# A planner that orders one fused kernel's operations by passes from the front and from the back in turn

## The chip, the cores and the metric

The kernel runs on one core of a Trainium2 chip. The metric is the device time of one execution in microseconds. A core has five engines with an instruction stream each: TensorE (PE; its weight loads are listed as PEld), VectorE (DVE), ScalarE (ACT), GpSimd (POOL) and SyncE (SP). SP issues all transfers here. Each engine works through its stream in order, and a semaphore wait holds up whatever stands behind it on that engine.

## The reference

Three stages follow each other. All are in 32-bit floats at the end; the kernel gets weights as 64-bit floats and splits them.

```python
# attention: 4 batches, 8 heads, 576 tokens, head size 64, window of 64 tokens
scores = (1 / 8) * q @ k.T            # kept where 0 <= i - j < 64
attn = exp(scores - max); attn = attn / (sum(attn) + 1e-9)
x = attn @ v                          # 2304 tokens x 512
# first block, 512 -> 2048 -> 512
h = x @ w_in
g = (a0 + a1 h + a2 h^2 + a3 h^3) / (1 + |b0| |h| + |b1| h^2 + 1e-6)
x = g @ w_out
# second block, 512 -> 1024 -> 1024 -> 512
out = (((x @ w1) * (x @ w2)) @ w3) @ w_out2
```

## The kernel before, in words

Tokens are cut into six blocks of 384 (index j). Attention runs in 48 steps of one token range and one pair of heads; a step multiplies scores (S, L516), masks and reduces them on VectorE (L519), takes the exponential on ScalarE (L525), scales each row by the reciprocal sum (nm, L530 on ScalarE or, in the first eight steps, L532 on GpSimd), transposes (T, L537), copies the transposed tile (ac, L541) and multiplies by v (O, L482); the result is split into two parts of fewer bits for TensorE (L487, L490).

The first block runs over 48 pairs of 128-wide chunks of its 2048 inner columns: product H (L600), the rational function on ScalarE and VectorE (L612 to L671), product D into the four accumulators of the token block (L677). Each product is three matmuls of split parts. The chunk pairs go through the halves of the inner columns in a fixed order of turns (L247): blocks 0, 1, 2 with the first half, then 2, 1, 0 with the second, then blocks 3 to 5 with both.

Every weight tile arrives as 64-bit floats in 512 KB (`conv`, load L378), is converted by three bit operations on VectorE (L382, L385, L388), and is split by ScalarE (L395) and VectorE (L398). The second block has the products AB (L843), a product of its last two weights W (L878), its result for the first token pair (L1129), and for the other two token pairs products P and R by a scheme of seven block products (L1029, L1174).

None of these loops sets the order in which engines work. Each operation is registered with a planner (class `Plan`, L33): a key, the engines that may do it with a planned cost for each ("E" TensorE, "V" VectorE, "A" ScalarE, "P" GpSimd, "D" the transfer queue), the operations that it follows, the buffers that it takes or uses, and a `tail`, the planned delay until its result can be used. `order` (L70) turns these into one sequence:

1. Due times are worked out backwards over the dependences from a nominal sequence of TensorE's products (`seq`), by costs, tails and a lag between engines.
2. In each buffer ring the values are ordered by those due times (L111), and each new value has to follow the users of the value whose buffer it takes.
3. Due times are worked out again with these dependences, and the operations are placed by one pass from the front: whenever an engine is free in the plan, it takes the ready operation that is due first. VectorE's operations marked `port` and all of GpSimd's exclude each other.

The operations are then issued in the order of their planned starts. The chip keeps each engine's order, but starts each instruction when its semaphores allow, so the plan's times themselves are not used on the chip. An operation of "D" occupies the planned transfer queue for its cost, one after the other, and its result is usable a tail later.

Of the kernel before, what the change touches and what calls it, by code (L numbers as in the profile page):

```python
# [19 lines left out]
P = 128  # L20
B, H, S, D = 4, 8, 576, 64
# [18 lines left out]
class Plan:  # L40
# [29 lines left out]
    def order(self):  # L70
        ops, n = self.ops, len(self.ops)
        preds = [[(self.index[k], True) for k in o["after"]] for o in ops]

        def topo():
            left = [len(p) for p in preds]
            succs = [[] for _ in ops]
            for i, p in enumerate(preds):
                for j, _ in p:
                    succs[j].append(i)
            out = [i for i in range(n) if not left[i]]  # L80
            for i in out:
                for j in succs[i]:
# [12 lines left out]
        def lag(i, j):  # L95
            a, b = ops[i]["engines"][0][0], ops[j]["engines"][0][0]
            return self.SAME[a] if a == b else self.CROSS

        def dues():
            out, succs = topo()  # L100
            due = [1e9] * n
            for i in reversed(out):
                d = min([due[j] - lag(i, j) - ops[i]["engines"][0][1] - ops[i]["tail"] for j in succs[i]], default=1e9)
                due[i] = d if ops[i]["due"] is None else min(d, ops[i]["due"])
            return due

        due = dues()

        tags = {}
        for v, (a, users) in self.values.items():  # L110
            tags.setdefault(v[0], []).append((due[a] if ops[a]["turn"] is None else ops[a]["turn"], a, users))  # L111
        for tag, vs in tags.items():
            vs.sort()
            for k in range(1, len(vs)):
                preds[vs[k][1]].append((vs[k - 1][1], False))
                if k >= self.rings[tag]:
                    preds[vs[k][1]] += [(u, True) for u in vs[k - self.rings[tag]][2]]
        due = dues()
        _, succs = topo()
        left = [len(p) for p in preds]  # L120
        ready_at = [0.0] * n
        free = {}
        pend, ready = {}, {}
        for o in ops:
            for e, _ in o["engines"]:
                free[e] = 0.0
                pend[e], ready[e] = [], []
        start = [None] * n
        events = [0.0]

        def release(i):
            for e, _ in ops[i]["engines"]:
                heappush(pend[e], (ready_at[i], i))
            heappush(events, ready_at[i])

        for i in range(n):
            if not left[i]:
                release(i)
        port = 0.0
        while events:  # L140
            t = heappop(events)
            for e in free:
                while pend[e] and pend[e][0][0] <= t:
                    i = heappop(pend[e])[1]
                    if start[i] is None:
                        heappush(ready[e], (due[i], i))
            while True:
                best = None
                for e in free:
                    if free[e] > t:  # L150
                        continue
                    kept = []
                    while ready[e]:
                        d, i = ready[e][0]
                        if start[i] is not None:
                            heappop(ready[e])
                        elif port > t and self.ports(ops[i], e):
                            kept.append(heappop(ready[e]))
                        else:
                            if best is None or d < best[0]:  # L160
                                best = (d, i, e)
                            break
                    for x in kept:
                        heappush(ready[e], x)
                if best is None:
                    break
                _, i, e = best
                o = ops[i]
                o["engine"], start[i], free[e] = e, t, t + dict(o["engines"])[e]
                heappush(events, free[e])  # L170
                if self.ports(o, e):
                    port = free[e]
                for j in succs[i]:
                    left[j] -= 1
                for j in set(succs[i]):
                    real = any(r for k, r in preds[j] if k == i)
                    ej = ops[j]["engines"][0][0]
                    d = free[e] + o["tail"] + (self.SAME[e] if e == ej else self.CROSS) if real else t + 1e-6
                    ready_at[j] = max(ready_at[j], d)
                    if not left[j]:  # L180
                        release(j)
        assert all(s is not None for s in start)
        self.start = start
        return [ops[i] for i in sorted(range(n), key=lambda i: (start[i], i))]
# [3 lines left out]
def body(ctx: ExitStack, tc: tile.TileContext, qkv, w_in, w_out, a, b, w1, w2, w3t, wo2, out):  # L188
# [43 lines left out]
    op = plan.op  # L232
# [134 lines left out]
    def conv(name, dst, n, src, tag, due=None, spare=False, pre=None, kept=None):  # L367
# [40 lines left out]
        op((name, n, "load"), (("D", 1.55),), load, after=["swap"] if spare else [], new=(ws,), tail=2.2, due=due)  # L408
# [6 lines left out]
        else:  # L415
            op((name, n, "hi"), (("A", 0.52),), hi, after=((name, n, "b2"),), uses=(wt, ws))
            op((name, n, "lop"), (("V", 0.61),), lo, port=True, after=((name, n, "hi"),), uses=(wt, ws), due=pre + 30.0)
            op((name, n, "keep"), (("D", 1.55),), keep, after=((name, n, "lop"),), uses=(ws,), tail=2.0, due=pre + 31.0)
            op((name, n, "lo"), (("D", 1.55),), again, after=((name, n, "keep"),), new=(wc,), tail=2.2)
# [14 lines left out]
        op((name, n, "keepb"), (("D", 0.8),), keepb, after=((name, n, "b2"),), uses=(wt,), tail=2.0, due=None if pre is None else pre + 30.5)  # L434
        op((name, n, "keepw"), (("D", 1.55),), keepw, after=((name, n, "lo"),), uses=(wc,), tail=2.0)
# [20 lines left out]
    def attn(pair):  # L456
# [35 lines left out]
        def step(k):  # L492
# [51 lines left out]
            op(("load", i), (("D", 1.0),), load, new=(kb_, qb), tail=2.2)  # L544
            op(("loadv", i), (("D", 0.6),), loadv, after=(("load", i),), new=(vb,), tail=2.2)
# [33 lines left out]
    for m in range(2):  # L579
        after = [("xl", i) for i in range(0, 2 * NP, 2) if i % NP // 2 == m]  # L580
        op(("spill", m), (("D", 2.4),), lambda _, m=m: spill(m), after=after, uses=(("x0", 0),), tail=2.2, due=seq["H", HALF - 2, 0])
        after, xb = [("spill", m)] + [("fill", 0)] * m, ("x0", AGAIN)
        op(("fill", m), (("D", 2.4),), lambda _, m=m: fill(m), after=after, new=() if m else (xb,), uses=(xb,) if m else (), tail=2.2)
# [140 lines left out]
    def evacuate(j, part, then):  # L724
# [30 lines left out]
        for n in range(NK):  # L755
# [8 lines left out]
            if more:  # L764
                after.append(("evl", j, n // 2))
                if n % 2 == 0:
                    op(("evl", j, n // 2), (("D", 1.2),), lambda _, n=n: load(n), after=(("store", j, 0, n), ("store", j, 0, n + 1)), new=(vb,), tail=2.2)
            new = new and not more
            op(("ev", *key), (("A", 0.48), ("V", 0.46))[more:], lambda e, n=n: copy(n, e), after=after, new=(vb,) if new else (), uses=((f"acc{n}", (j, part)),) + (() if new else (vb,)), due=due)
            op(("store", *key), (("D", 0.6),), lambda _, n=n: store(n), after=(("ev", *key),), uses=(vb,), tail=2.0)  # L770
# [33 lines left out]
    def x2_load(j):  # L804
# [15 lines left out]
        for n in range(NK):  # L820
            eb = ("xe", ("x2", j, n))
            after = [("store", j, int(j < HALVED), n), "swap"] + ([("x2l", j, n - 1)] if n else [])
            op(("x2l", j, n), (("D", 0.6),), lambda _, n=n: load(n), after=after, new=(eb,) if n else (eb, xb), uses=(xb,) if n else (), tail=2.2)
# [115 lines left out]
    def tokens(u):  # L939
# [24 lines left out]
        for i, (b, (k, h)) in enumerate(where.items()):  # L964
            j = 2 * u + h
            op(("xl2", u, b), (("D", 1.2),), lambda _, b=b: load(b), after=["swap2"] + [("store", j, int(j < HALVED), n) for n in (2 * k, 2 * k + 1)], new=(fb[b],), tail=2.2, turn=seq["P", u, 0, 1] - 20.0 + i)
        seven((u,), f, fb, {b: ("xl2", u, b) for b in where}, split)

    def weights(u, n):
# [34 lines left out]
        for i in range(4 if u > 1 else 2):  # L1004
            after = [(("w1", "w2")[i], n, "keepw")] if i < 2 else [("keeps", n, i - 2)]
            op(("sw", u, n, i), (("D", 1.55),), lambda _, i=i: load(i), after=after, new=(wbs[i],), tail=2.2)
        if u > 1:
            return
        op(("bs", n), (("D", 1.55),), loadb, after=(("w1", n, "keepb"), ("w2", n, "keepb")), new=(bb,), tail=2.2)
        for i in range(4):  # L1010
            op(("sum", n, i), (("V", 0.34),), lambda _, i=i: sums(i), port=True, after=[("sum", n, i - 1)] if i else [("bs", n)], new=() if i else (sb,), uses=(bb, sb) if i else (bb,))
        for q in range(2):
# [3 lines left out]
            op(("keeps", n, q), (("D", 1.55),), lambda _, q=q: keep(q), after=(("sw", u, n, 2 + q),), uses=(wb,), tail=2.0)  # L1016
# [103 lines left out]
    def result0(h):  # L1120
# [23 lines left out]
        for n in range(NK):  # L1144
            pb, sb = (f"acc{n}", ("R0", h, n)), ("wt", ("so", h, n))
            op(("so", h, n), (("A", 0.45),), lambda _, n=n: copy(n), after=(("R0", h, 3, n),), new=(sb,), uses=(pb,), due=seq["R0", h, 3, n] + 2.0)
            op(("out", h, n), (("D", 0.6),), lambda _, n=n: store(n), after=(("so", h, n),), uses=(sb,), tail=2.0)

    def result(u):
# [53 lines left out]
        for n in range(2):  # L1203
# [5 lines left out]
            for t, half, h, k in (("p1", 0, 0, "p1"), ("u2", 0, 1, "c12"), ("p1b", 1, 0, "p1b"), ("u3", 1, 1, "c22")):  # L1209
                op(("out", u, n, t), (("D", 0.6),), lambda _, t=t, half=half, h=h, n=n: store(t, n, half, h), after=(K(k, n),), uses=(tb(t, n),), tail=2.0)  # L1210
# [79 lines left out]
```

## Time and profile before

| | us |
|---|---|
| median of 3 runs (lowest, highest) | 843.84 (842.42, 844.37) |
| the profiled execution | 843.9 |
| its span, first to last instruction | 842.0 |
| TensorE busy in the span | 811.6 |
| VectorE busy | 679.5 |
| ScalarE busy | 539.8 |

Busy time is the union of an engine's instruction times. The span is what the views of the trace cover, and the time of the run is longer by what lies before and after it. A wait is put down to the instruction that ended last before the waiting one could start. Granted clock 1.00 means TensorE's full clock, 2.4 GHz, and 0.50 half of it.

### The profile page before, as it was taken

How to read it: one execution, taken by the hardware profiler on the slowest of the kernel's cores; microseconds unless marked ns; L12 is line 12 of the kernel's file. 1: busy time of each engine (PE TensorE's matmuls, PEld its weight loads, DVE VectorE, ACT ScalarE, POOL GpSimd, SP SyncE). 2: the span in 40 equal slices, each digit the busy share in tenths (PEclk: the TensorE clock that was granted, in tenths of full speed). 3: DMA queues.
4: the chain of work that ended last, by engine and by line, in shares of the span. 5: the costliest groups of instructions: out<-in, count | busy, mean ns of one | idle time of the engine just before them, and what ended most of it. 6: DMA issues, size and time to landing. Idle time of an engine off the chain costs nothing.

```text
span 842.0 us, 14037 instructions
## 1 busy us (share of the span) xinstructions
PE 811.6 (96%) x5088; PEld 784.0 (93%) x5088; DVE 679.5 (81%) x1333; ACT 539.8 (64%) x1213; POOL 31.7 (4%) x42
## 2 busy tenths in 40 slices
PE   5699989999999999999999999999999999999998
PEld 4589979899999999999999999999889999999998
DVE  6789999999977799888889999889857358933554
ACT  6799888677777978778758685333444335542334
POOL 2100000000001000000000002000000000000000
PEclk9699999999999999999999999999999999999999
DMA  7985472341305354212107856945336589537802
GB/s 243 290 293 162 131 221 100 113 132 47 123 20 164 122 184 159 67 53 89 51 11 249 304 188 224 290 161 192 128 112 236 181 293 307 203 120 252 302 3 76
DMA packets 61285, 138.81 MB, mean 165 GB/s; under 512 B 6944, under 2 KB 36640, under 8 KB 61216
## 3 DMA queue, kind: packets, MB, share of 16 engines
q1 hardware_dynamic: 61216, 137.92, 49.3%
q8 instruction: 40, 0.66, 0.3%
q14 instruction: 29, 0.24, 0.1%
HBM read 102.24 MB, written 35.65 MB: 164 GB/s over the span
## 4 chain that ended last, share of the span: by engine, by line
PE 73%; DVE 16%; ACT 4%; DMA 4%; issue 2%; POOL 1%; SPq 0%; DVEq 0%; ACTq 0%; POOLq 0%
PE acc L677 17%; PE hp L600 14%; PE ab L843 7%; PE pb L1029 6%; PE wp L878 5%; PE pc L1029 4%; PE pa L1029 4%; PE po L1129 4%; PE pb L1174 3%; PE sp L516 3%; PE pc L1174 2%; PE pa L1174 2%; DVE qa L661 2%; DVE wt L385 1%; DVE wt L388 1%
## 5 line engine op out<-in xcount | busy, mean ns | idle before, releaser
L600 PE MATMUL hp<-x,wc 128*128 128x384 f32 x1152 | 219.5, 339 | 1.4 <-DVE x L490 0.4
L677 PE MATMUL acc<-g,wc 128*128 128x384 f32 x1152 | 211.9, 337 | 6.1 <-DVE g L671 3.5
L677 PEld LDWEIGHTS acc<-g,wc 128*128 128x128 f32 x1152 | 198.8, 188 | 11.1 <-DVE g L671 5.0
L600 PEld LDWEIGHTS hp<-x,wc 128*128 128x128 f32 x1152 | 198.9, 188 | 3.7 <-ACT bl L633 2.0
L617 ACT ACTIVATE qa<-hp,cb 128x384 f32<-128x384 f32 x96 | 55.7, 580 | 55.3 <-PE hp L600 54.3
L622 ACT ACTIVATE u<-hp,ca 128x384 f32<-128x384 f32 x96 | 64.9, 676 | 5.9 <-PE hp L600 5.9
L395 ACT ACTIVATE wc<-wt 128x512 fp32r<-128x512 f32 x68 | 42.5, 632 | 40.9 <-DVE wt L388 40.7
L843 PE MATMUL ab<-x,wc 128*128 128x384 f32 x384 | 67.8, 334 | 0.0
L843 PEld LDWEIGHTS ab<-x,wc 128*128 128x128 f32 x384 | 66.7, 188 | 0.0
L525 ACT ACTIVATE sm<-sm,st 128x128 f32<-128x128 f32 x144 | 56.6, 399 | 11.8 <-DVE st L519 11.2
L637 DVE SCALAR_TENSOR_TENSOR qa<-h,cab,qa 128x768 f32<-128x768 f32 x48 | 48.9, 1019 | 15.2 <-ACT h L612 15.1
L1029 PE MATMUL pb<-xb,wc 128*128 128x384 f32 x288 | 56.3, 334 | 0.0
L516 PE MATMUL sp<-k,q 128*128 128x128 f32 x288 | 44.1, 304 | 12.6 <-DMA k<-in_qkv 7.4
L516 PEld LDWEIGHTS sp<-k,q 128*128 128x128 f32 x288 | 41.2, 216 | 13.9 <-DVE st L519 4.5
L641 ACT ACTIVATE r<-qa,cq 128x768 f32<-128x768 f32 x48 | 45.2, 942 | 13.8 <-DVE qa L637 10.2
L1040 DVE TENSOR_TENSOR u<-u,pc 128x384 f32<-128x384 f32 x32 | 17.7, 552 | 43.6 <-ACT u L1037 32.0
L1029 PEld LDWEIGHTS pb<-xb,wc 128*128 128x128 f32 x288 | 50.5, 188 | 0.0
L385 DVE SCALAR_TENSOR_TENSOR wt<-ws,wt 128x512 uint32<-128x512 uint32 x72 | 49.3, 688 | 0.5
L388 DVE SCALAR_TENSOR_TENSOR wt<-ws,wt 128x512 uint32<-128x512 uint32 x72 | 49.3, 686 | 0.3
L612 ACT ACTIVATE h<-hp 128x384 f32<-128x384 f32 x96 | 46.7, 486 | 2.9 <-DVE u L625 2.9
L398 DVE TENSOR_TENSOR wc<-wt,wc 128x512 fp32r<-128x512 f32 x68 | 46.3, 684 | 1.2 <-ACT wc L395 1.2
L1110 DVE TENSOR_TENSOR rt<-prod,rt 128x768 fp32r<-128x768 f32 x36 | 34.3, 954 | 15.0 <-ACT rt L1107 14.9
(97 smaller groups left out, 1344.6 us busy)
## 6 DMA issues: line engine op xcount, KB each, us to landing
wc<-kw SPq DMA_DIRECT2D x48, 512.0 KB, 5.0
kw<-wc SPq DMA_DIRECT2D x32, 512.0 KB, 5.6
q<-in_qkv SPq DMA_DIRECT2D x48, 192.0 KB, 3.3
v<-in_qkv SPq DMA_DIRECT2D x48, 192.0 KB, 3.0
ws<-in_w_in SPq DMA_DIRECT2D x16, 512.0 KB, 4.3
ws<-in_w_out SPq DMA_DIRECT2D x16, 512.0 KB, 4.3
ws<-in_w SPq DMA_DIRECT2D x16, 512.0 KB, 4.4
ws<-in_w3t SPq DMA_DIRECT2D x16, 512.0 KB, 4.3
```

The source lines that it names most:

```text
L385: stt(out=x["b"], in0=x["st"][:, :, 0], scalar=29, in1=x["b"], op0=ALU.logical_shift_right, op1=ALU.bitwise_or)
L388: stt(out=x["b"], in0=x["st"][:, :, 1], scalar=0xC0000000, in1=x["b"], op0=ALU.bitwise_and, op1=ALU.bitwise_or)
L516: nc.tensor.matmul(sp[:, w, :], x["q"][:, w], x["k"][:, w * W_:w * W_ + P], start=True, stop=True)
L525: act(x["sm"][:, m, :], x["sm"][:, m, :], AF.Exp, bias=col(0, k, m), scale=-1.0, accum_out=col(1, k, m))
L600: nc.tensor.matmul(x["hp", m], win[f0 + m][:, s_, kk * P:(kk + 1) * P], (xh, xl)[m_][xk][:, kk, :], start=(kk == 0 and i == 0), stop=(kk = ...
L617: act(x["qa"][:, m, :], x["hp", m], AF.Abs, scale=b0)
L622: act(x["u"][:, m, :], x["hp", m], AF.Identity, scale=a3, bias=a2)
L637: stt(out=x["qa"], in0=x["h2"], scalar=b1, in1=x["qa"], op0=MUL, op1=ADD)
L677: nc.tensor.matmul(accs[j, part, n], wout[f0 + m][:, s_, n * P:(n + 1) * P], x["g"][:, m_, m, :], start=(first and i == 0), stop=(last and ...
L843: nc.tensor.matmul(x[m], w_[n][:, s_, kk * P:(kk + 1) * P], x2[j][m_][:, kk, :], start=(kk == 0 and i == 0), stop=(kk == NK - 1 and i == 2))
L1029: nc.tensor.matmul(x[m], sws[u, n, i0][:, s_, (c0 + k) * P:(c0 + k + 1) * P], t[:, m_, k, :], start=(first and k == 0 and i == 0), stop=(k ...
L1174: nc.tensor.matmul(x[m, n], w[:, s_, (c + n) * P:(c + n + 1) * P], rts[u, b, r][:, m_, k, :], start=(first and r == 0 and k == 0 and i == ...
```

## The change

`order` gets an argument `rounds` of 16. Due times and the buffer order are worked out as before. Then a pass from the front is made as before, and in each round a pass from the back: the same placing routine on reversed dependences, with each operation on the engine that the pass from the front gave it, taking first the operation that ended last. Its mirrored start times become the due times of the next pass from the front. Of the 17 passes from the front, the one with the shortest planned length gives the order and the engines. Beside that, the planned costs of the transfers are changed, all by about a tenth.

```diff
-    def order(self):
+    def order(self, rounds=16):
...
+        first = dues(base)
+        preds = buffers(lambda a: first[a] if ops[a]["turn"] is None else ops[a]["turn"])
+        due = dues(preds)
+        best = None
+        for r in range(rounds + 1):
+            _, succs = topo(preds)
+            start, took = run(preds, succs, due)
+            end = [s + dict(o["engines"])[e] for o, s, e in zip(ops, start, took)]
+            length = max(e + o["tail"] for o, e in zip(ops, end))
+            if best is None or length < best[0]:
+                best = length, start, took
+            self.trail = getattr(self, "trail", []) + [length]
+            if r == rounds:
+                break
+            back, _ = run(succs, preds, [-e for e in end], took)
+            due = [-b - dict(o["engines"])[e] for o, b, e in zip(ops, back, took)]
+        _, self.start, took = best
...
-        op((name, n, "load"), (("D", 1.55),), load, after=["swap"] if spare else [], new=(ws,), tail=2.2, due=due)
+        op((name, n, "load"), (("D", 1.72),), load, after=["swap"] if spare else [], new=(ws,), tail=2.2, due=due)
...
-            op(("load", i), (("D", 1.0),), load, new=(kb_, qb), tail=2.2)
-            op(("loadv", i), (("D", 0.6),), loadv, after=(("load", i),), new=(vb,), tail=2.2)
+            op(("load", i), (("D", 1.1),), load, new=(kb_, qb), tail=2.2)
+            op(("loadv", i), (("D", 0.66),), loadv, after=(("load", i),), new=(vb,), tail=2.2)
```

The other transfers follow the same pattern: 512 KB from 1.55 to 1.72, the two-tile loads and stores of a token block from 2.4 to 2.6, 384 KB from 1.2 to 1.3, 256 KB from 0.8 to 0.88, 192 KB from 0.6 to 0.66. The two constants stay at 0.95, and so do all tails and all engine costs.

## Rows read from the trace of the kernel before

**Rows 1.** Page, part 1: busy us, share of the span, instructions
```profile
PE 811.6 (96%) x5088; PEld 784.0 (93%) x5088; DVE 679.5 (81%) x1333; ACT 539.8 (64%) x1213; POOL 31.7 (4%) x42
```

**Rows 2.** Busy time by stretch, columns in the first row
```profile
core 0: us, PE busy (x) PEld busy (x) DVE busy (x) ACT busy (x) POOL busy (x), PEclk, DMA share, GB/s
0.00:21.00 21.00, 12.02 (x84) 9.89 (x84) 13.19 (x52) 13.05 (x46) 4.86 (x17) 1.00 0.76 243
21.00:42.00 21.00, 14.17 (x108) 11.81 (x108) 15.94 (x58) 14.91 (x53) 3.30 (x5) 0.67 0.94 290
42.00:63.00 21.00, 19.14 (x141) 16.92 (x142) 18.50 (x53) 20.28 (x63) 1.98 (x2) 0.92 0.83 294
63.00:210.00 147.00, 140.74 (x945) 134.96 (x944) 145.65 (x307) 119.32 (x287) 9.89 (x10) 1.00 0.40 129
...
253.00:337.00 84.00, 82.99 (x621) 79.98 (x620) 72.51 (x177) 70.52 (x188) 5.96 (x6) 1.00 0.47 158
...
463.00:547.00 84.00, 83.26 (x478) 82.36 (x477) 80.43 (x124) 51.54 (x92) 5.69 (x2) 1.00 0.76 251
...
631.00:673.00 42.00, 40.87 (x235) 40.62 (x235) 23.60 (x45) 18.86 (x34) 0.00 (x0) 1.00 0.62 210
...
800.00:842.00 42.00, 38.53 (x223) 38.21 (x221) 20.86 (x27) 16.23 (x26) 0.00 (x0) 0.99 0.11 39
```

**Rows 3.** VectorE's waits, 0 to 63 us: total us, times, longest
```profile
DVE wt L382 <- DMA ws<-in_w_out: 3.4, 1, 3.4
...
DVE wt L382 <- DMA ws<-in_w_in: 2.0, 1, 2.0
DVE sm L519 <- ACT wc L395: 1.9, 1, 1.9
DVE u L625 <- ACT u L622: 1.7, 1, 1.7
DVE u L628 <- ACT h L612: 0.4, 1, 0.4
```

**Rows 4.** TensorE's waits, 63 to 210 us
```profile
PE acc L677 <- DVE g L671: 2.5, 4, 1.1
PE acc L677 <- POOL g L671: 1.7, 2, 1.2
PE op L482 <- DVE st L519: 1.1, 1, 1.1
```

**Rows 5.** Timelines of VectorE and TensorE: start, us, instruction, [idle before]
```profile
23.91 0.43 DVE L382 TENSOR_SCALAR wt<-ws 128x512 uint32<-128x512 uint32 x1 [3.39 <-DMA ws<-in_w_out]
...
24.87 1.62 PE L516 MATMUL sp<-k,q 128*128 128x128 f32 x6 [4.42 <-DVE st L519]
```

**Rows 6.** Timeline of the transfer queue, first and last of 23 issues
```profile
0.74 0.39 SPq L502 DMA_DIRECT2D q<-in_qkv  x1
...
16.76 0.38 SPq L378 DMA_DIRECT2D ws<-in_w_out  x1
```

**Rows 7.** Chain that ended last, one piece: start, us, what
```profile
16.76 7.13 DMA ws<-in_w_out
```

**Rows 8.** Busy time by 4 us windows, columns as in Rows 2
```profile
8.00:12.00 4.00, 1.44 (x6) 1.35 (x6) 3.79 (x14) 2.22 (x9) 0.23 (x1) 1.00 0.99 344
...
28.00:32.00 4.00, 3.25 (x18) 2.48 (x19) 2.09 (x4) 3.54 (x12) 1.54 (x2) 0.50 0.96 256
...
48.00:52.00 4.00, 3.23 (x16) 2.14 (x15) 3.17 (x7) 4.00 (x16) 0.00 (x0) 1.00 1.06 369
```

**Rows 9.** Scalings on GpSimd, and TensorE's waits for them
```profile
L532 POOL TENSOR_SCALAR sm<-sm,st 128x128 f32<-128x128 f32 x10 | 6.1, 622 | 27.1 <-DVE st L475 18.6 <-DVE st L519 8.5
...
PE tp L537 <- POOL sm L532: 1.8, 4, 0.7
```

More of the change, by code (lines that the diff above doesn't have):

```diff
@@ L93, in topo, with lag, dues @@
             return out, succs
[L95 to L100, printed above, removed]
+        def lag(i, j, e=None):
+            a, b = e or ops[i]["engines"][0][0], ops[j]["engines"][0][0]
+            return ops[i]["tail"] + (self.SAME[a] if a == b else self.CROSS)
+        def dues(preds):
+            out, succs = topo(preds)
             due = [1e9] * n
@@ L102, in dues @@
             for i in reversed(out):
-                d = min([due[j] - lag(i, j) - ops[i]["engines"][0][1] - ops[i]["tail"] for j in succs[i]], default=1e9)
+                d = min([due[j] - lag(i, j) - ops[i]["engines"][0][1] for j, _ in succs[i]], default=1e9)
                 due[i] = d if ops[i]["due"] is None else min(d, ops[i]["due"])
             return due
[L107 to L148, printed above, removed]
-                for e in free:
[L150 to L158, printed above, removed]
-                        else:
[L160 to L181, printed above, removed]
@@ L182, in order, with buffers @@
-        assert all(s is not None for s in start)
-        self.start = start
-        return [ops[i] for i in sorted(range(n), key=lambda i: (start[i], i))]
+        def buffers(due):
+            preds = [list(p) for p in base]
+            tags = {}
+            for v, (a, users) in self.values.items():
+                tags.setdefault(v[0], []).append((due(a), a, users))
+            for tag, vs in tags.items():
+                vs.sort()
+                for k in range(1, len(vs)):
+                    preds[vs[k][1]].append((vs[k - 1][1], False))
+                    if k >= self.rings[tag]:
+                        preds[vs[k][1]] += [(u, True) for u in vs[k - self.rings[tag]][2]]
+            return preds
@@ new lines, in run, with release @@
+        def run(preds, succs, due, fixed=None):
+            left = [len(p) for p in preds]
+            ready_at = [0.0] * n
+            free, pend, ready = {}, {}, {}
+            for o in ops:
+                for e, _ in o["engines"]:
+                    free[e] = 0.0
+                    pend[e], ready[e] = [], []
+            start, took = [None] * n, [None] * n
+            events = [0.0]
+            def release(i):
+                for e, _ in ops[i]["engines"] if fixed is None else ((fixed[i], 0),):
+                    heappush(pend[e], (ready_at[i], i))
+                heappush(events, ready_at[i])
+            for i in range(n):
+                if fixed is not None:
+                    ready_at[i] = ops[i]["tail"]
+                if not left[i]:
+                    release(i)
+            port = 0.0
+            while events:
+                t = heappop(events)
+                for e in free:
+                    while pend[e] and pend[e][0][0] <= t:
+                        i = heappop(pend[e])[1]
+                        if start[i] is None:
+                            heappush(ready[e], (due[i], i))
+                while True:
+                    best = None
+                    for e in free:
+                        if free[e] > t:
+                            continue
+                        kept = []
+                        while ready[e]:
+                            d, i = ready[e][0]
+                            if start[i] is not None:
+                                heappop(ready[e])
+                            elif port > t and self.ports(ops[i], e):
+                                kept.append(heappop(ready[e]))
+                            else:
+                                if best is None or d < best[0]:
+                                    best = (d, i, e)
+                                break
+                        for x in kept:
+                            heappush(ready[e], x)
+                    if best is None:
+                        break
+                    _, i, e = best
+                    cost = dict(ops[i]["engines"])[e]
+                    took[i], start[i], free[e] = e, t, t + cost
+                    heappush(events, free[e])
+                    if self.ports(ops[i], e):
+                        port = free[e]
+                    for j, real in succs[i]:
+                        left[j] -= 1
+                        if fixed is None:
+                            d = free[e] + lag(i, j, e) if real else t + 1e-6
+                        else:
+                            d = free[e] + lag(j, i, fixed[j]) if real else free[e] - dict(ops[j]["engines"])[fixed[j]] + 1e-6
+                        ready_at[j] = max(ready_at[j], d)
+                        if not left[j]:
+                            release(j)
+            assert all(s is not None for s in start)
+            return start, took
@@ L187, in body @@
+        _, self.start, took = best
+        for o, e in zip(ops, took):
+            o["engine"] = e
+        return [ops[i] for i in sorted(range(n), key=lambda i: (self.start[i], i))]
 @with_exitstack
@@ L417, in conv @@
             op((name, n, "lop"), (("V", 0.61),), lo, port=True, after=((name, n, "hi"),), uses=(wt, ws), due=pre + 30.0)
[L418 to L419 removed]
+            op((name, n, "keep"), (("D", 1.72),), keep, after=((name, n, "lop"),), uses=(ws,), tail=2.0, due=pre + 31.0)
+            op((name, n, "lo"), (("D", 1.72),), again, after=((name, n, "keep"),), new=(wc,), tail=2.2)
         if kept is None:
@@ L580, in body @@
         after = [("xl", i) for i in range(0, 2 * NP, 2) if i % NP // 2 == m]
-        op(("spill", m), (("D", 2.4),), lambda _, m=m: spill(m), after=after, uses=(("x0", 0),), tail=2.2, due=seq["H", HALF - 2, 0])
+        op(("spill", m), (("D", 2.6),), lambda _, m=m: spill(m), after=after, uses=(("x0", 0),), tail=2.2, due=seq["H", HALF - 2, 0])
         after, xb = [("spill", m)] + [("fill", 0)] * m, ("x0", AGAIN)
-        op(("fill", m), (("D", 2.4),), lambda _, m=m: fill(m), after=after, new=() if m else (xb,), uses=(xb,) if m else (), tail=2.2)
+        op(("fill", m), (("D", 2.6),), lambda _, m=m: fill(m), after=after, new=() if m else (xb,), uses=(xb,) if m else (), tail=2.2)
     win, wout, accs = {}, {}, {}
@@ L822, in x2_load @@
             after = [("store", j, int(j < HALVED), n), "swap"] + ([("x2l", j, n - 1)] if n else [])
-            op(("x2l", j, n), (("D", 0.6),), lambda _, n=n: load(n), after=after, new=(eb,) if n else (eb, xb), uses=(xb,) if n else (), tail=2.2)
+            op(("x2l", j, n), (("D", 0.66),), lambda _, n=n: load(n), after=after, new=(eb,) if n else (eb, xb), uses=(xb,) if n else (), tail=2.2)
             op(("x2h", j, n), (("A", 0.45),), lambda _, n=n: hi(n), after=(("x2l", j, n),), uses=(eb, xb))
@@ L965, in tokens @@
             j = 2 * u + h
-            op(("xl2", u, b), (("D", 1.2),), lambda _, b=b: load(b), after=["swap2"] + [("store", j, int(j < HALVED), n) for n in (2 * k, 2 * k + 1)], new=(fb[b],), tail=2.2, turn=seq["P", u, 0, 1] - 20.0 + i)
+            op(("xl2", u, b), (("D", 1.3),), lambda _, b=b: load(b), after=["swap2"] + [("store", j, int(j < HALVED), n) for n in (2 * k, 2 * k + 1)], new=(fb[b],), tail=2.2, turn=seq["P", u, 0, 1] - 20.0 + i)
         seven((u,), f, fb, {b: ("xl2", u, b) for b in where}, split)
@@ L1146, in result0 @@
             op(("so", h, n), (("A", 0.45),), lambda _, n=n: copy(n), after=(("R0", h, 3, n),), new=(sb,), uses=(pb,), due=seq["R0", h, 3, n] + 2.0)
-            op(("out", h, n), (("D", 0.6),), lambda _, n=n: store(n), after=(("so", h, n),), uses=(sb,), tail=2.0)
+            op(("out", h, n), (("D", 0.66),), lambda _, n=n: store(n), after=(("so", h, n),), uses=(sb,), tail=2.0)
     def result(u):
@@ L1209, in result @@
             for t, half, h, k in (("p1", 0, 0, "p1"), ("u2", 0, 1, "c12"), ("p1b", 1, 0, "p1b"), ("u3", 1, 1, "c22")):
-                op(("out", u, n, t), (("D", 0.6),), lambda _, t=t, half=half, h=h, n=n: store(t, n, half, h), after=(K(k, n),), uses=(tb(t, n),), tail=2.0)
+                op(("out", u, n, t), (("D", 0.66),), lambda _, t=t, half=half, h=h, n=n: store(t, n, half, h), after=(K(k, n),), uses=(tb(t, n),), tail=2.0)
     for n in range(NG):
```

26 lines of the change are left out of this document (14 added, 12 removed).

## The prediction, made before the changed kernel ran

> **What bounds the kernel now.** I read the engine shares first, then the busy times by stretch, then the waits of VectorE and TensorE in the early stretches, then single instructions. TensorE is busy 811.6 of 842.0 us and VectorE 679.5 [rows 1]: on average the matrix engine is the limit, and only 30.4 us of its time are idle. The stretches [rows 2] show where. In 0 to 63 us TensorE idles 8.98 + 6.83 + 1.86 = 17.67 us; in 63 to 210 us 6.26 us; in three later stretches 1.01 + 0.74 + 1.13 = 2.88 us; in the last 42 us 3.47 us. That is 30.28 of the 30.4. All other stretches after 210 us are full. An order of the same operations can remove idle time and nothing else, so the pool is these four amounts.
>
> What sets the early idle time is not TensorE. In 63 to 210 us VectorE is busy 145.65 of 147 us [rows 2], and what ends TensorE's waits there is VectorE's or GpSimd's last step of a chunk and one softmax step (2.5, 1.7 and 1.1 us, [rows 4]). VectorE has to convert the weights, run softmax and evaluate the rational function for everything that TensorE multiplies before about 210 us. As long as it is full, another order only moves the waits about. The part that an order can give back is VectorE's own idle time ahead of it: in 0 to 63 us 7.81 + 5.06 + 2.50 = 15.37 us [rows 2]. Of that, waits for the first weights (2.0), a late weight transfer (3.4), a ScalarE copy (1.9) and two ScalarE outputs of the first chunk (1.7 and 0.4) are named [rows 3]; the rest is mostly before any score exists.
>
> The last 3.47 us are the final addition and store behind the last matmul: the same operations stand there in any order. I count nothing.
>
> **The change part by part.** Nothing is removed or added on the chip: instruction counts, tiles and bytes stay. Two things move the instructions: the sixteen rounds, and the transfer durations in the plan. The buffer order inside each ring is still set once, from the first due times, so the sequence of chunks on the accumulators and of weights in their rings stays; what can move is how the streams interleave on each engine and on the one queue that issues all transfers (SP's), and which of two engines takes an operation.
>
> *Transfers, planned longer.* The clearest loss is VectorE's conversion at 23.91 us, which waits 3.39 us for weights; the softmax step behind it in program order, and the scores behind that on TensorE, wait too (4.42 us, [rows 5]). The transfer was issued at 16.76 us and took 7.13 us [rows 6, 7]. By 16.76 us the queue had issued, this one included, 12 q and k transfers (6 planned operations), 4 of v, the two constants (one operation) and 5 of weights: 23 issues, of which the first and the last are shown [rows 6]. The old plan prices them at 6 x 1.0 + 4 x 0.6 + 0.95 + 5 x 1.55 = 17.10 us, so from 0.74 us and with its 2.2 us of tail it lands at 20.04 at the latest; the new prices give 6 x 1.1 + 4 x 0.66 + 0.95 + 5 x 1.72 = 18.79 us, landing 21.73. The chip landed it at 16.76 + 7.13 = 23.89. So the new durations close 1.69 of a gap of 3.85 us, 44%. A plan that expects the transfer 1.69 us later puts other VectorE work ahead of the conversion; 44% of the 3.39 us is 1.5 us, my value. Bounds: 0 (the same order comes out) and 3.4 (all of it); I stay near the middle because that is how far the prices go.
>
> Is 1.72 us for 512 KB truer than 1.55? The queue moved 243 to 294 GB/s in the three early stretches [rows 2], which for 512 KB is 524 / 294 = 1.78 us, against 338 GB/s for 1.55 us and 305 GB/s for 1.72; but in 4 us windows with all engines filled it moved 344, 256 and 369 GB/s [rows 8]. So the new figure is the better mean, the old one the better peak. The Trainium skill, page "DMA: Bandwidth & Descriptors", section "Where 436 GB/s comes from", speaks against the edit: it puts a core's memory limit at about 358 GB/s, which would be an estimated 1.46 us for 512 KB, below even the old price. The trace's 369 GB/s window agrees with the page and its 294 GB/s stretch does not; by that rule the first term is 0.
>
> *Passes from the back and from the front.* The first pass takes due times from chains of latency alone: ten conversions due at once look equally urgent. The pass from the back packs each engine and so gives each operation the latest start that its engine allows. In the early stretches this should order VectorE and ScalarE better: the waits 1.9 + 1.7 + 0.4 = 4.0 us [rows 3] are ScalarE doing something less urgent first. Bounds: 0 (ScalarE is 20.28 of 21 busy in 42 to 63 us, [rows 2]) to 4.0; half is 2.0 us, as one of the two large waits lies in that full stretch and the other not.
>
> *63 to 210 us.* VectorE's 1.35 us idle is all that an order can take there; bounds 0 to 1.35, below zero if VectorE stalls anew. I take 0.
>
> *After 210 us.* The passes can close holes: 2.88 us, in 463 to 547 us with VectorE at 80.43 of 84 us [rows 2], so not there; of the others I take half of 1.01 and half of 1.13, about 1.0 us. Bounds: 2.88, and a loss of as much, if the tight places move. In the other stretches TensorE is full, has no hole to give and is covered from below: VectorE and ScalarE are far from full there, so an operation that starts a microsecond later costs nothing.
>
> Sum: 1.5 + 2.0 + 0 + 1.0 = 4.5 us off the profiled span of 842.0, giving 837.5. Around the span lie 843.9 - 842.0 = 1.9 us, so 839.4 us; the profiled execution (843.9) stands at the median of the runs (843.84).
>
> **Rivals.**
> 1. *The planned gain is all the change does; the chip doesn't follow.* The early kernel is limited by how much VectorE work must precede 210 us: 13.19 + 15.94 + 18.50 + 145.65 = 193.3 us of it. If its idle time only changes place, the time stays at 843.8. For it: 99% in 63 to 210 us. Against it: the named waits of 9.4 us before that.
> 2. *The page's rule.* Weights land sooner than planned in calm windows, the first term is 0 and the rest holds: 842.0 - 3.0 + 1.9 = 840.9. For it the 344 and 369 GB/s windows, against it the stretch means. This sum is the main one less the 1.5 us, whoever states the rule.
> 3. *Slower: GpSimd takes more of the early softmax scalings.* The plan prices one at 0.35 us there and 0.32 on ScalarE, for the first eight steps (24 operations). On the chip GpSimd's ten took 622 ns each in the mean, and TensorE waited four times for them, 1.8 us in all, 0.45 us each [rows 9]. A pass that counts ScalarE as full gives GpSimd the remaining 14: up to 14 x 0.45 = 6.3 us on the chain from score to first chunk. Taking 10 of the 14: 4.5 us, 848.4. It decides when the count on GpSimd passes about 20 (ten more eat the 4.5 us of gain). Against it: the plan still thinks ScalarE the quicker.
> 4. *Much faster.* The early VectorE idle time falls to what stands before the first score, about 5.5 us (the 2.0 us wait included): 15.37 - 5.5 = 9.9 us, and 1.0 us later: 842.0 - 10.9 + 1.9 = 833.0. For it: the passes repeat until the plan is shortest. Against it: the plan does not know the landing of 7.13 us.
>
> **How the numbers follow.** The forecast, 839.4, has a chance of 0.38 with its own range of 837 to 842; rival 1 0.17, rival 2 0.10, rival 3 0.20, rival 4 0.15. Runs of this kernel spread over 842.4 to 844.4, so under 0.2%, 1.7 us, I call it no change. Faster: 0.38 + 0.10 + 0.15 less a little that ends at the bound, 0.61; same: most of rival 1 and that little, 0.16; slower: rival 3 and the rest of rival 1, 0.23. The range takes in rival 4 in part (831 if 2 us more goes) and most of rival 3: 831 to 847.5.
>
> **What would show it.** Right: VectorE's idle time in 0 to 63 us falls from 15.37 to about 12, no wait of 3 us for weights, TensorE's idle time there from 17.7 to about 14, the first chunk's product starting some 3 us earlier, and stretches after 210 us still full. Rival 1: VectorE waits elsewhere by as much. Rival 3: more than ten scalings on GpSimd and waits of the transposes behind them. The forecast is wrong, too, if TensorE has new holes after 210 us: then the pass from the back has packed something against a need that comes later on the chip than in the plan.

## The result, and the profile after

The changed kernel takes 834.67 us in the median of four runs, the kernel before 843.50 beside it: ratio 0.9895, 95% interval 0.9874 to 0.9916. A later comparison (e7 below) gave 833.88 for 842.76, 0.990 [0.9878, 0.9921]. It is faster, as forecast, but by 8.8 us where 4.5 were forecast. The profiled execution took 833.71 us, its span 831.9.

Page of the changed kernel, part 1, then its busy time by stretch (columns as in [rows 2]):

```profile
PE 807.9 (97%) x5088; PEld 783.1 (94%) x5088; DVE 680.2 (82%) x1331; ACT 537.5 (65%) x1212; POOL 37.8 (5%) x45
```

```profile
0.00:21.00 21.00, 11.62 (x84) 9.39 (x84) 13.53 (x58) 13.64 (x48) 4.94 (x17) 0.92 0.85 282
21.00:42.00 21.00, 16.49 (x138) 13.73 (x138) 19.25 (x63) 17.54 (x62) 2.84 (x6) 0.92 0.86 294
42.00:63.00 21.00, 16.02 (x115) 14.77 (x116) 19.45 (x52) 18.37 (x56) 1.98 (x2) 0.84 0.85 272
63.00:210.00 147.00, 145.84 (x979) 141.01 (x978) 145.29 (x294) 120.19 (x284) 11.72 (x10) 1.00 0.41 131
...
253.00:337.00 84.00, 83.89 (x622) 81.39 (x621) 74.73 (x169) 71.80 (x191) 4.00 (x4) 1.00 0.46 151
...
463.00:547.00 84.00, 83.67 (x482) 83.10 (x481) 81.39 (x130) 48.88 (x87) 7.97 (x2) 1.00 0.75 255
...
631.00:673.00 42.00, 42.00 (x245) 42.00 (x244) 20.05 (x39) 17.69 (x32) 0.00 (x0) 1.00 0.86 281
...
800.00:832.00 32.00, 28.46 (x165) 28.13 (x163) 17.53 (x21) 13.78 (x21) 0.00 (x0) 1.00 0.13 50
```

Against [rows 2]: TensorE's idle time in 0 to 63 us did not fall, 9.38 + 4.51 + 4.98 = 18.87 us for 17.67. VectorE's did: 7.47 + 1.75 + 1.55 = 10.77 for 15.37. In 63 to 210 us TensorE idles 1.16 us for 6.26, with VectorE as full as before and a granted clock of 1.00 in both kernels, so the clock is no part of that gain. The later holes fell from 2.88 to 0.11 + 0.33 + 0 = 0.44 us, the end stayed (3.54 for 3.47).

Busy time hides stalls inside the pipeline, so I also sum for every matmul the time to the next one's start, less the pace of its kind where nothing waits (0.1734 us for 384 columns). This excess, with the wait for the first operand, was 40.5 us before 210 us and 4.9 after it, and became 33.9 and 1.4: 6.6 us won early, 3.5 late, together the 10.1 us between the two spans. Of the early part all but 0.4 lies in 63 to 210 us. TensorE's busy time itself fell, from 811.6 to 807.9 us for the same 5088 matmuls: 3.7 of the 10.1 us come out of time that counts as busy.

VectorE's waits in 0 to 63 us, and TensorE's in 63 to 210 us, of the changed kernel (in us, times, longest):

```profile
DVE sm L547 <- PE sp L544: 3.7, 4, 2.3
DVE mask L474 <- POOL mask L472: 2.5, 1, 2.5
DVE wt L410 <- DMA ws<-in_w_in: 1.8, 2, 1.4
DVE x L518 <- ACT x L515: 1.1, 2, 0.8
DVE sm L547 <- ACT sm L553: 0.4, 1, 0.4
DVE g L686 <- ACT r L672: 0.3, 1, 0.3
DVE wt L410 <- DMA ws<-in_w_out: 0.3, 1, 0.3
```

```profile
PE acc L705 <- DVE g L699: 0.6, 1, 0.6
PE hp L628 <- DVE x L518: 0.2, 1, 0.2
```

The 3.4 us wait for weights is 0.3. The 1.9 and 1.7 us waits for ScalarE are gone [rows 3], though others came, 1.8 us in all for 4.0. The waits for the chunk's last step [rows 4] fell from 4.2 us to 0.6. The first chunk's product (first row before, second row after) started 5.6 us earlier, where some 3 were expected. That is not where the time comes from, since it starts at 33.6 us in e1 below too, which gains 1 us:

```profile
39.42 2.37 PE L600 MATMUL hp<-x,wc 128*128 128x384 f32 x12
...
33.81 2.36 PE L628 MATMUL hp<-x,wc 128*128 128x384 f32 x12
```

### The profile page after: what moved, and what is told of

Same layout as the page of the kernel before. It is cut to its first block, busy times and chain, and to the rows that moved or that the text cites. A ratio compares the mean times of both kernels' runs of the same rounds, so it can differ in the third digit from the quotient of the medians.

```text
span 831.9 us, 14053 instructions
## 1 busy us (share of the span) xinstructions
PE 807.9 (97%) x5088; PEld 783.1 (94%) x5088; DVE 680.2 (82%) x1331; ACT 537.5 (65%) x1212; POOL 37.8 (5%) x45
## 4 chain that ended last, share of the span: by engine, by line
PE 76%; DVE 15%; DMA 4%; issue 2%; ACT 1%; SPq 1%; POOL 1%; DVEq 0%; POOLq 0%
PE acc L705 18%; PE hp L628 16%; PE ab L871 8%; PE pb L1057 6%; PE wp L906 5%; PE po L1157 4%; PE pc L1057 4%; PE pa L1057 4%; PE pb L1202 3%; PE pc L1202 2%; PE pa L1202 2%; PE sp L544 2%; DMA ws<-in_w_out 2%; DVE wt L413 1%; DVE qa L689 1%
## 5 line engine op out<-in xcount | busy, mean ns | idle before, releaser
L705 PE MATMUL acc<-g,wc 128*128 128x384 f32 x1152 | 216.2, 338 | 4.3 <-POOL g L699 2.9
L628 PEld LDWEIGHTS hp<-x,wc 128*128 128x128 f32 x1152 | 201.6, 190 | 2.7 <-DVE x L518 1.5
L544 PE MATMUL sp<-k,q 128*128 128x128 f32 x288 | 41.9, 290 | 9.5 <-DMA k<-in_qkv 5.1
L1135 ACT ACTIVATE rt<-prod 128x768 fp32r<-128x768 f32 x36 | 30.0, 844 | 31.0 <-PE po L1157 9.0
L1068 DVE TENSOR_TENSOR u<-u,pc 128x384 f32<-128x384 f32 x32 | 17.7, 552 | 39.5 <-ACT u L1065 30.2
L544 PEld LDWEIGHTS sp<-k,q 128*128 128x128 f32 x288 | 38.9, 202 | 11.0 <-DMA q<-in_qkv 4.0
```

Of the source, the lines that this page charges most:

```text
L544: nc.tensor.matmul(sp[:, w, :], x["q"][:, w], x["k"][:, w * W_:w * W_ + P], start=True, stop=True)
L628: nc.tensor.matmul(x["hp", m], win[f0 + m][:, s_, kk * P:(kk + 1) * P], (xh, xl)[m_][xk][:, kk, :], start=(kk == 0 and i == 0), stop=(kk = ...
L705: nc.tensor.matmul(accs[j, part, n], wout[f0 + m][:, s_, n * P:(n + 1) * P], x["g"][:, m_, m, :], start=(first and i == 0), stop=(last and ...
```

## Experiments

Every ratio is against the kernel before on the same chip, with its 95% interval; waits and busy times are from one profiled execution of each. The theory at the outset was that VectorE's supply sets TensorE's pace up to about 210 us; the main rival, that what counts is what stands before what.

**Which part of the change, e1 to e4.** One line of `order` or the durations:

```diff
-    def order(self, rounds=16):
+    def order(self, rounds=0):      # e1; e3: rounds=1
...
-(("D", 1.72),)
+(("D", 1.55),)                      # e2, all transfers as before; e4: all x 1.1, 1.892
```

> The new transfer durations with the one pass from the front (rounds = 0), so the durations alone. Theory of the forecast (the durations make the plan expect weights later, so VectorE stalls less early on): the 3.39 us wait for weights shrinks, 1.5 us faster, 842.0. Rival A (the passes do nearly all, the durations only make the plan longer and change the order at random): no gain, 842.5 to 846, with a wait for weights of 3 us still there or another in its place. Rival B (the durations do most): 836 to 838.

841.83 us, 0.9987 [0.9975, 0.9998]: about 1.1 us faster (0.2 to 2.1), near the 1.5 of the forecast. The wait for w_out weights fell from 3.4 to 1.9 us:

```profile
DVE wt L410 <- DMA ws<-in_w_out: 1.9, 2, 1.4
```

> The old transfer durations with the 16 rounds, so the passes alone. Forecast's theory, parts that add up: 834.7 + 1.5 = 836.2. Rival A (passes do all): 834 to 835.5. Rival B (durations do most): 841 or more. Rival C (each helps only with the other, as the passes pack the transfers so tightly that the old durations mislead): 838 to 841, with waits for weights or for q, k, v above those of the changed kernel.

838.27 us, 0.9946 [0.9925, 0.9967], and unsteady: 834.0 to 842.6 in twelve runs. The passes alone give about 4.5 us; 4.5 + 1.1 is 3.2 short of what both together give, with an uncertainty of some 2.7 us from the three intervals. The median lies in rival C's range. Its sign was waits for weights or for q, k, v above those of the changed kernel: VectorE's for weights were not above them (1.8 and 0.3), but TensorE's for k were. Below is e2, then two profiles of the changed kernel, the first one and e7:

```profile
PE sp L544 <- DMA k<-in_qkv: 12.5, 7, 4.3
...
PE sp L544 <- DMA k<-in_qkv: 5.1, 2, 3.6
...
PE sp L544 <- DMA k<-in_qkv: 9.0, 5, 3.7
```

The same order differs by 3.9 us from one profile to the next, and the profiled execution of e2 is one of its longer ones (840.95), so rival C is neither shown nor ruled out.

> The new durations with one round: one pass from the front, one from the back, one more from the front. The planned length is 837.2 us for the first pass, 831.9 after one round and 823.7 after sixteen. If the chip follows the planned length, it gets (837.2 - 831.9) / (837.2 - 823.7) = 39% of what the sixteen rounds give over none. If instead what matters is that due times know the load of each engine at all, which the first round brings, it gets nearly all of it, 835 to 836.5. If the lengths below 1% are chance: anything between 834 and 844 with no relation.

839.13 us, 0.9957 [0.9941, 0.9973]: 38% of the way from e1 (841.83) to the changed kernel (834.67), where 39% was the planned share. The interval of e3 alone allows 19 to 57%, so the near match is in part luck; it does rule out that one round gives nearly all. By places the shares are quite unlike 39%: late, one round closed the whole excess (4.1 to -0.1 us, table below); early, it lost 3.1 us (39.0 to 42.1).

> All transfer durations another tenth longer (512 KB 1.89 us), sixteen rounds; planned length 828.7. If weights that land later than planned were what is left in the early stretches, this is faster than the changed kernel: 832 to 834. If transfers are no longer the limit, the longer durations only hold VectorE's conversions back: 835 to 839.

837.49 us, 0.9935 [0.9918, 0.9952]: another tenth costs about 3 us. The fences are from e1, e3 and e4 in turn, each with a row for 0 to 210 us and one for 210 to 800:

```profile
0.00:210.00 210.00, 181.99 (x1285) 171.64 (x1286) 195.22 (x474) 168.43 (x449) 18.05 (x33) 0.99 0.52 175
210.00:800.00 590.00, 587.27 (x3598) 573.20 (x3598) 465.21 (x838) 355.00 (x740) 8.57 (x8) 1.00 0.51 170
```

```profile
0.00:210.00 210.00, 182.66 (x1267) 171.07 (x1268) 192.17 (x457) 164.22 (x435) 24.85 (x40) 0.98 0.53 174
210.00:800.00 590.00, 589.99 (x3622) 577.74 (x3621) 468.17 (x849) 357.80 (x751) 16.30 (x10) 1.00 0.51 171
```

```profile
0.00:210.00 210.00, 186.22 (x1269) 177.73 (x1270) 191.78 (x451) 164.36 (x436) 27.31 (x40) 0.94 0.54 175
210.00:800.00 590.00, 589.91 (x3623) 577.86 (x3622) 470.41 (x853) 357.01 (x752) 13.86 (x10) 1.00 0.51 170
```

Without passes TensorE idles 590 - 587.27 = 2.73 us in 210 to 800 us; after one round 0.01. One round closes the late holes. Before 210 us e3 and e4 have less VectorE work done (192.2 and 191.8 us) than e1 (195.2), and TensorE fewer matmuls (1267 and 1269 for 1285).

**Load or order, e5, e6, e9, with e7 as the control.**

```diff
+        EIGHT = {("wout", 2), ("wout", 3), ("win", 6), ("win", 7), ("wout", 4), ("wout", 5), ("wout", 6), ("wout", 7)}
         def b1_(_):
+            if key in EIGHT:
+                return              # e5, in the kernel before; e6, in the changed one: the operation once more
```

> The kernel before, in its own order, without one of VectorE's bit operations (about 0.6 us each) in the 9th to 16th weight conversion, which stand between 42 and 97 us: 8 x 0.6 = 4.8 us of VectorE left out, and with it the three lowest bits of those weights' mantissas. Theory (VectorE's supply limits TensorE up to about 210 us, so time saved on VectorE early is paid out as waits that TensorE does not have at 105 to 210 us): TensorE's excess over its pace before 210 us falls by 4 to 5 us, the kernel by as much, 838 to 839. Rival (the waits come from the order on VectorE, urgent work behind less urgent work, and not from its load): less than 1.5 us, 841.5 or more.

842.36 us, 0.9995 [0.9982, 1.0007]: no change. Busy time of e5, columns as before:

```profile
0.00:21.00 21.00, 12.46 (x84) 10.52 (x84) 12.40 (x51) 13.09 (x46) 4.17 (x17) 0.84 0.74 235
21.00:42.00 21.00, 13.53 (x108) 11.06 (x108) 15.80 (x59) 14.43 (x52) 3.30 (x5) 0.76 0.91 296
42.00:63.00 21.00, 17.88 (x142) 15.76 (x143) 17.36 (x51) 20.43 (x64) 1.97 (x2) 1.00 0.84 297
63.00:105.00 42.00, 41.89 (x336) 40.19 (x336) 40.60 (x105) 38.10 (x109) 1.98 (x2) 1.00 0.49 152
105.00:210.00 105.00, 99.37 (x621) 95.75 (x617) 103.78 (x199) 81.31 (x181) 7.89 (x8) 1.00 0.37 123
```

The eight operations left out took 8 x 0.69 = 5.5 us on the chip, not the 4.8 reckoned. VectorE idles 8.60 + 5.20 + 3.64 + 1.40 = 18.84 us before 105 us, where the kernel before idled 15.54. Of these 3.3 us, 0.9 lie before 40.3 us, where the first of the eight stands in the kernel before; the other 2.4 are left-out time that turned into waiting. The rest was filled with other work, and the kernel gained nothing from it in that order.

> The changed kernel in its own order, with the same bit operation done twice in the 9th to 16th weight conversion: 4.8 us of VectorE more, same result. Theory of VectorE's supply: TensorE loses 3 to 5 us before 210 us, 838 to 839.5, and the waits come back at 105 to 210 us. Rival (order, not load): less than 1.5 us, 836 at most.

> The changed kernel once more, on the chip of the two runs above, as what e6 and e8 are to be held against. It was 834.7 in four runs within 2.2 us; the passes with the old durations spread over 834 to 842.6 in twelve. If the changed kernel is as unsteady, its median rises to 836 or 837 here; otherwise it stays within 834 to 835.5.

e6 839.07 us, 0.9950 [0.9933, 0.9967]; e7 833.88, just under its expected range, in six runs from 831.6 to 836.7: 5.5 us more on VectorE (the doubled operation, first row below) cost 5.2 us, about one for one. The changed kernel has no slack there: load counts where VectorE is kept fed. The waits came back, but mostly in 42 to 105 us rather than where I expected them (TensorE's excess in 63 to 105 us 3.0 us for 0.7 in the changed kernel, in 105 to 210 us unchanged). The next two rows are from e6, the last is from the changed kernel:

```profile
L416 DVE SCALAR_TENSOR_TENSOR wt<-ws,wt 128x512 uint32<-128x512 uint32 x8 | 5.5, 687 | 0.1
...
42.00:63.00 21.00, 15.03 (x108) 13.67 (x109) 20.26 (x56) 18.68 (x57) 1.97 (x2) 0.84 0.82 258
63.00:105.00 42.00, 40.41 (x303) 37.68 (x302) 41.25 (x100) 36.90 (x101) 5.56 (x5) 1.00 0.44 148
...
63.00:105.00 42.00, 41.95 (x335) 39.66 (x333) 40.63 (x106) 39.28 (x110) 6.15 (x6) 1.00 0.47 152
```

> The kernel before (one pass, old durations), with the due times written by hand taken off the weight loads of the second half of the inner columns (they still set the ring order). In VectorE's order the 17th to 32nd conversion then stand behind 6, 6, 7, 8, 8, 9, 10, 11, 11, 12, 13, 14, 15, 15, 16, 17 chunk pairs, as in the changed kernel, where before they stand behind 5, 6, 6, 7, 7, 8, 9, 10, 10, 12, 12, 12, 13, 14, 15, 16. Theory (the conversions stood in the way of urgent chunk work on a full VectorE, and the passes move them back): TensorE's excess at 105 to 210 us falls from 8.4 us to 3 to 5, the kernel to 837.5 to 840. Rival (their place does not matter; the passes gained by VectorE's idle time before 63 us alone): 842 to 843.5. Rival (conversions now come late for the second half): 844 or more, with waits for converted weights at 175 to 215 us.

The edit gives the load `due=None` and `turn=due` for these 16 tiles. 841.74 us, 0.9988 [0.9975, 1.0001], at most 2 us, and TensorE idles 6.01 us in 105 to 210 us where the kernel before idled 5.48: moving conversions alone does not do it.

**The plan's costs and its length, e8, e10 to e14.**

```diff
-(("A", 0.32), ("P", 0.35)) if i < 8
+(("A", 0.32), ("P", 0.62)) if i < 8           # e8, e10, e12, e14; e13: 0.58
-engines = (("V", 0.47), ("P", 0.97))[:2 if j < G else 1]
+engines = (("V", 0.47), ("P", 1.05))[:2 if j < G else 1]     # all but e10
-op(("x2", j, n), (("V", 0.47), ("P", 0.97))
+op(("x2", j, n), (("V", 0.47), ("P", 3.0))                   # all but e10
# beside that, transfers 1% shorter in e12, 1% longer in e13, 3% longer in e14; rounds=24 in e13, e14
```

> The changed kernel with GpSimd's planned costs as the trace has them (scaling 0.62 us for 0.35, the split of a chunk 1.05 for 0.97, of the second block's input 3.0 for 0.97); planned length 822.9 for 823.7. If the plan's error in these costs holds the early stretches back (TensorE waits 2.9 us for GpSimd at the first product with w_out), 831 to 833. If the early waits come from elsewhere, the order is merely another one: 834 to 839.

828.36 us, 0.9831 [0.9814, 0.9847]: the fastest, 14 us under the kernel before and below both ranges that I had expected.

> Of the three GpSimd costs of the 828.4 us kernel only that of the softmax scaling (0.62 us for 0.35) in the changed kernel; planned length 824.0. If this one is what helps: 828 to 830. If the other two are, or all three: 832 to 836.

> Only the other two GpSimd costs (split of a chunk 1.05 for 0.97, of the second block's input 3.0 for 0.97); planned length 827.1, the longest of the three. If the true price of the split helps, by taking away the 2.9 us wait at the first product with w_out: 829 to 831. If time follows the planned length: 837.

e10 830.20 us, 0.9849 [0.9828, 0.9870]; e11 834.46, 0.9899 [0.9879, 0.9918]. With these durations the price of the scaling brings nearly all of e8's gain and the other two prices none. e11 fits neither of its two expectations.

> All three GpSimd costs as in the 828.4 us kernel, with the transfer durations 1% shorter, which is no truer and no less true: planned length 827.9 for 822.9. If the true costs make the order good, 828 to 831. If the planned length decides, 5 us more at the slope seen so far (half of it), 831. If the order is luck, anything from 828 to 840.

837.47 us, 0.9931 [0.9913, 0.9949]. Transfers 1% shorter in the plan, and 9 us are lost, where the planned length grew by 5 and the slope seen before would have made it 2.5. So the prices that I had called true do not protect.

> The kernel of 828.4 us with the scaling on GpSimd at 0.58 us for 0.62, transfers 1% longer and 24 rounds: of 36 such settings the one with the shortest plan, 822.3 us. If the planned length decides: 827 to 831. If the settings as such decide (true GpSimd prices): 828 to 832 too; told apart by e14. If chance beyond the plan decides: anywhere from 828 to 839.

> The kernel of 828.4 us with transfers 3% longer and 24 rounds; planned length 828.7 us, the longest of 36 such settings. If the planned length decides: 837 to 840, with VectorE's busy time before 210 us at 194 us or below, for 198.3 in the kernel of 828.4. If the true prices decide: 828 to 833.

e13 831.34 us, 0.9870 [0.9850, 0.9891]; e14 837.61, 0.9934 [0.9909, 0.9960]. Prices nearly alike, 6 us apart, as the planned lengths are. But e13, planned 0.6 us shorter than e8, came out 3 us longer. VectorE's busy time before 210 us in e8, e13 and e14:

```profile
0.00:210.00 210.00, 190.72 (x1336) 181.67 (x1337) 198.33 (x470) 173.84 (x458) 25.65 (x40) 0.98 0.54 177
```

```profile
0.00:210.00 210.00, 192.98 (x1338) 183.22 (x1339) 197.79 (x478) 174.10 (x463) 24.52 (x38) 0.99 0.53 177
```

```profile
0.00:210.00 210.00, 186.38 (x1290) 176.89 (x1291) 193.14 (x458) 166.44 (x443) 18.33 (x31) 0.97 0.54 177
```

All orders together (excess and VectorE from the profiled execution, us; e5 and e6 are left out, since they change the work):

| | planned length | measured | VectorE busy before 210 | TensorE's excess before 210 | 210 to 800 |
|---|---|---|---|---|---|
| before | 833.7 | 842.8 | 193.3 | 40.5 | 4.9 |
| e1 | 837.2 | 841.8 | 195.2 | 39.0 | 4.1 |
| e3 | 831.9 | 839.1 | 192.2 | 42.1 | -0.1 |
| e4 | 828.6 | 837.5 | 191.8 | 41.6 | -0.2 |
| e14 | 828.7 | 837.6 | 193.1 | 38.1 | 0.2 |
| e12 | 827.9 | 837.5 | 194.2 | 39.3 | 0.0 |
| e11 | 827.1 | 834.5 | 196.5 | 35.9 | 0.1 |
| e2 | 825.8 | 838.3 | 194.5 | 39.0 | 3.5 |
| e10 | 824.0 | 830.2 | 199.0 | 31.6 | 1.3 |
| after (e7) | 823.7 | 833.9 | 199.0 | 32.1 | 1.2 |
| e8 | 822.9 | 828.4 | 198.3 | 30.1 | -0.2 |
| e13 | 822.3 | 831.3 | 197.8 | 29.8 | 1.4 |

Three things can be read from it. The late excess is 3.5 us or more in the plans without passes (e9 too, 4.4) and in e2, and at most 1.4 in the others. The early excess goes with the time that VectorE works before 210 us: over these twelve, the changed kernel's first profile and e9, a line has a slope of -1.6 us per us (correlation -0.94). That does not say which drives which, since a kernel whose TensorE is further on by 210 us has by then also given VectorE more to do. The measured time goes with the planned length (correlation 0.88), with misses of up to 4 us (e2).

## Why the prediction was wrong

The direction was right. Of the places, the stretches after 210 us were, with too small a size; TensorE won nothing in 0 to 63 us, where two terms were put, and most in 63 to 210 us, put at nothing.

*The pool.* "An order of the same operations can remove idle time and nothing else" failed: 3.7 of the 10.1 us of span came out of TensorE's busy time, 811.6 to 807.9 us. The four amounts of idle time were not all that there was to win.

*Transfers, 1.5 us.* Right in size: durations alone gave 1.1. The wait fell to 1.9 us with them and to 0.3 with the passes. But longer is not better as such, since another tenth lost 3 us (e4). By the rule of the Trainium skill (page "DMA: Bandwidth & Descriptors", section "Where 436 GB/s comes from"), a limit of about 358 GB/s, this term is 0; the interval of e1 leaves 0 out, but barely, and the 369 GB/s window of [rows 8] that the prediction calls in agreement with that rule lies above its limit.

*Better order early, 2.0 us.* VectorE's two long waits for ScalarE went, as said. With the transfers I expected its idle time to fall from 15.37 to about 12; it fell to 10.77 (10.3 to 11.0 in e7, e8, e10 and e13). But TensorE's idle time in that stretch, which this term was to shorten, did not fall.

*63 to 210 us: "I take 0".* This step failed most. I reasoned that a full VectorE leaves nothing to win there, and set its own 1.35 us of idle time as the bound. TensorE's idle time there fell by 5.1 us and its excess by 6.2, with VectorE just as full in both kernels (145.65 and 145.29 us); what changed is what VectorE has done before. The 4.6 us of its idle time that went before 63 us did not shorten TensorE's waits there, where I looked for them (17.7 to about 14; it was 18.87). They went into work done ahead, conversions among it (12 done by 63 us, where 10 were), and TensorE's waits fell later. That the one paid for the other is argued from e6 and the table; no run isolates it.

What a microsecond of VectorE is worth stays open: 6.6 us for 4.6 here and a slope of 1.6 across the orders, but only 5.2 us for 5.5 in e6, the one run that changes VectorE's load in an order that keeps it fed. More than one for one would fit the plan's costs, in which a chunk pair is 48 matmuls, 8.3 us of TensorE, for about 6.6 us of VectorE; e6 speaks against it.

*After 210 us, 1.0 us.* Too small: 2.4 us of idle time and 3.5 us of excess, more than the 2.88 us that I had set as the bound. I had ruled out 463 to 547 us because VectorE is nearly full; e3 shows TensorE idle 0.01 us in all of 210 to 800 us, with the same operations. A nearly full engine is no proof that the order on it is the best.

*Rivals.* 1 falls (ratio interval below 1). Its premise was that the chip doesn't follow the plan; yet the plan's own gain, 833.7 to 823.7 us, was nearer to the measured 8.8 us than the sum was (plans with different prices compare only roughly: e1's is 3.5 us longer and the chip 1.1 us faster). 2 is 1.5 us further off than the forecast. 3 falls: eleven scalings on GpSimd for ten, and TensorE waited less than 1 us for them; but that price does weigh in the plan (e10). 4 was nearer the measured time than the forecast, but by luck: it has VectorE's early idle time fall to 5.5 us, and that stayed at 10.77. The time of e8 lies below it.

*What stays open.* e5 and e6 do not agree with a plain load limit: VectorE's load counts where the order keeps it fed (e6), and freeing it helps nothing where the order doesn't (e5). So the link of the table is between TensorE and VectorE's time in use; what makes one order use it better than another was not isolated. Nor was the cause of the 3.2 us by which both parts exceed their sum: with 1% of a duration worth 9 us (e8 and e12), it may be the luck of one order, or rival C of e2.

## What to carry to other kernels

An engine that is full is not thereby at its limit: look at how long it idled before, and count that time as something to win, beside its waits in the full stretch. What it is worth downstream has to be measured (one for one in e6). A planner that repeats passes from both ends closed nearly all holes in the calm stretches with one round, but in a crowded start its result jumps by several us for 1% in a cost, so generate many plans, look at the shortest, and measure a few of them: the shortest plan here (e13) was not the fastest kernel (e8).

## What was not expected of the hardware

The same order ran within 3.1 us in eleven runs of e1 (840.19 to 843.30) and over 8.6 us in twelve of e2 (833.96 to 842.57): how steady a run is differs from order to order, and why was not tested.

GpSimd's prices are not single numbers. Its split of a 128 x 384 tile took 1.10 us in the mean in the first block and 3.12 us for the second block's input, an instruction of the same shape that subtracts where the first multiplies. The second mean hides 1.33, 1.34 and 6.68 us, and in e8, planned with 3.0 us for it, the four that GpSimd did took 1.1 to 1.7 us. The scalings priced at 0.62 us had a median of 0.37 us in e8. Why one of them takes several times as long as the next is not shown. The rows are from the changed kernel, the last two from e8 (times in ns, lowest/median/highest, where three are given):

```profile
L699 POOL TENSOR_TENSOR g<-u,r 128x384 fp32r<-128x384 f32 x19 | 20.7, 1102 | 238.7 <-ACT h L640 78.6 <-DVE u L695 53.3 <-DVE u L693 41.6
...
L846 POOL TENSOR_TENSOR x<-x2f,x 128x384 fp32r<-128x384 f32 x3 | 9.3, 3120 | 217.1 <-ACT x L843 217.1
...
L846 POOL TENSOR_TENSOR x<-x2f,x x3: 1333/1344/6684, 446.4 to 514.3; 128x384 fp32r<-128x384 f32 x3
...
L846 POOL TENSOR_TENSOR x<-x2f,x x4: 1122/1562/1726, 503.9 to 513.7; 128x384 fp32r<-128x384 f32 x4
...
L560 POOL TENSOR_SCALAR sm<-sm,st x9: 367/371/688, 10.4 to 30.9; 128x128 f32<-128x128 f32 x9
```
